# A written order for VectorE and ScalarE in the expert part, and earlier tiles for the first block's second half

## The chip, the core and the metric

The kernel runs on one core of a Trainium2 chip. The metric is the device time of one execution in microseconds (us). The kernel uses all five engines of the core: TensorE (PE; its weight loads are listed as PEld), VectorE (DVE), ScalarE (ACT), GpSimd (POOL) and SyncE (SP), which issues nearly all DMAs here. Each engine works through its own queue of instructions, and semaphores order the engines among each other.

## What is computed

Causal attention over 4 batches, 8 heads, 576 tokens and a head width of 64, mixed with a recalled memory by a gate per head; the result, seen as 2304 tokens of width 512, goes through one gated feed-forward layer of width 1536 ("the expert part"):

```python
def _moe_ref(x, w_gate, w_val, w_out):
    g = x @ w_gate
    silu = g * (1.0 / (1.0 + np.exp(-g)))
    val = x @ w_val
    return (silu * val @ w_out).astype(np.float32)
```

The weights come as 64-bit words that the kernel turns into two 32-bit parts (a high and a low one), and the products are made of three matmuls each: high times high, high times low, low times high.

## The kernel before

**Attention.** A loop over 16 pairs of heads runs the steps named in `STEPS`. Its tiles lie in the pool `sb`, which closes when the loop is over. Each pair's result is stored to two arrays in DRAM, `xdh` and `xdl` (line 640); the last pair's second half is the last store. Beside the attention, `moe1` (lines 220 to 254) does the feed-forward part of four of the twelve weight slices (f = 0 to 3) for the first 1536 tokens. Its tiles are in the pool `mo`, the staging tiles of its weights in the pool `stg`.

**Expert part (from line 693).** Three blocks of 768 tokens, in the order 1536, 0, 768. Each block is two halves of 384 tokens. A unit is one weight slice f on one block. The first block has twelve units: eight plain ones for f = 0 to 3 and 8 to 11 (`eight`, 48 products and 18 sums of 3 products each into the output banks) and four by a seven-product scheme for f = 4 to 7 (`seven`, 42 products and 18). The two other blocks have eight units of `seven` each. So there are 28 units.

- `eight` makes four runs of 12 matmuls: half 0 gate, half 0 value, half 1 gate, half 1 value. Each run fills one of two ring banks in PSUM (tiles `g` and `m`). After a gate run ACT applies Silu (line 923), after a value run DVE multiplies (line 925), ACT rounds to the high part (line 885) and DVE makes the low part (line 114). In the first unit the runs are cut by the pairs of heads, in the order (0, 1), (2), (3), so that they can begin while the last pair is not stored.
- `direct` (line 799) loads the first unit's tokens: `p1` and `p2` are half 0 (tiles `xbh`, `xbl`), `p7` and `p4` are half 1 (tiles in the pool `mb`, which opens on line 781, after `sb` and `mo` are closed).
- `weights2` (line 708) turns a weight slice in three thirds. A third is: a load of 512 KB into one of two tiles `wrawb`, an ACT Prelu (line 714), three DVE operations (lines 715, 721, 722), and where the two parts are wanted at once an ACT copy (line 730) and a DVE subtraction. There are 24 thirds; the units 0 to 7 start three each.
- `operands` (line 744) makes the seven weight combinations of the next unit; `fetch` and `sums` (lines 789, 804) load the next block's tokens and add them; `spread` (line 815) splits the sums into high and low parts.

**What sets the order.** Tile, the planner, orders the instructions of each engine by their priority among those that are ready in its own estimate. The matmuls of the expert part are chained in program order (`inline`). The work of DVE and ACT is not: the conversion, the fetches and the operands have a priority that is later by `LATE` = 60 places, so they are put between the others where the planner sees room. Once planned, each engine runs its queue in that order.

Of the kernel before, what the change touches and what calls it, by code (L numbers as in the profile page):

```python
# [22 lines left out]
NF = DFF // 128  # L23
# [22 lines left out]
TURNS = (4, 5, 8, 9, 10, 11, 6, 7)  # L46
LATE = 60
# [16 lines left out]
def attention_moe(ctx: ExitStack, tc: tile.TileContext, qt, kt_, v, m, beta, wg, wv, wo, out):  # L64
# [135 lines left out]
    def up(ps, f, gv, xh, xl):  # L200
        hi, lo = wsplit[f]
        n = 0
        for kk in range(NPAIR):
            o = gv * 512 + (kk + 2 * gv) % 4 * 128
# [50 lines left out]

    xb = [xbp.tile([128, NPAIR, N2], F32R, name=f"xb{part}") for part in "hl"]
    mo = tc.tile_pool(name="mo", bufs=1, side="right", reuse_waits="tile")
    mo_pool = mo.__enter__()
    stg = tc.tile_pool(name="stg", bufs=1, side="right", reuse_waits="tile")
    stg_pool = stg.__enter__()  # L260
# [4 lines left out]
    with tc.tile_pool(name="sb", bufs=1, reuse_waits="tile") as sb:  # L265
# [385 lines left out]
        def fill(n, k):  # L651
            nonlocal done
            if k == 0:
                for f in WSTEP.get(n, ()):
                    for _ in weights(f, w1, stg_pool, "a", NRAW, 1, loads.get(AFTER[f])):
# [12 lines left out]
        for n in range(NP + 1):  # L668
# [20 lines left out]
        stg.__exit__(None, None, None)  # L689
# [4 lines left out]
    NU = 2 * N2  # L694
    with tc.tile_pool(name="w2", bufs=1, reuse_waits="tile") as w2, \
         tc.tile_pool(name="stg2", bufs=1, reuse_waits="tile") as stg2:
        later = list(range(FC1, NF))
        keep = {}
        for f in later:
            if f < NF - FC1:  # L700
                keep[f] = (
                    w2.tile([128, 1024], F32, name=f"wr{f}"), w2.tile([128, 512], F32R, name=f"woh{f}"),
                    w2.tile([128, 512], F32R, name=f"wol{f}"),
                )
# [3 lines left out]
        def weights2(f):  # L708
            for j, src in enumerate((wg, wv, wo)):
                raw = rot(stg2, "wrawb", [128, 512, 2], I32, 2)  # L710
                SP.dma_start(raw.rearrange("p a b -> p (a b)"), src[f].bitcast(I32))
                top, low = raw[:, :, 1], raw[:, :, 0]
                e = rot(stg2, "web", [128, 512], F32, 2)
                ACT.activation(e, top.bitcast(F32), AF.Prelu, scale=2.0**-111, alpha=2.0**32)  # L714
                DVE.tensor_scalar(e, e, W_TOP * 2.0**-111, -W_TOP * 2.0**-79, op0=ALU.min, op1=ALU.max)  # L715
                c = slice(j * 512, j * 512 + 512)
                if f in keep and j < 2:
                    a = keep[f][0][:, c].bitcast(I32)
                else:
                    a = rot(stg2, "wab", [128, 512], I32, 1)  # L720
                DVE.tensor_scalar(a, e.bitcast(I32), 3, None, op0=ALU.logical_shift_left)
                DVE.scalar_tensor_tensor(
                    out=a, in0=low, scalar=29, in1=a, op0=ALU.logical_shift_right, op1=ALU.bitwise_or
                )
                if f not in keep:
                    oh, ol = (x[:, c] for x in wsplit[f])
                elif j == 2:
                    oh, ol = keep[f][1:]
                if f not in keep or j == 2:
                    ACT.copy(oh, a.bitcast(F32))  # L730
                    split_lo(ol, a.bitcast(F32), oh)
                yield

        def more():
            for f in TURNS:
                yield from weights2(f)

        wgen = more()

        def convert(n):  # L740
            for _ in range(n):
                next(wgen, None)

        def operands(f):

            t = rot(stg2, "tt", [128, 1024], F32, 1)
            if f not in keep:
                bh, bl = wsplit[f]
                w = rot(stg2, "rb", [128, 1024], F32, 1)
                for c in (slice(0, 512), slice(512, 1024)):  # L750
                    DVE.tensor_tensor(w[:, c], bh[:, c].bitcast(F32), bl[:, c].bitcast(F32), op=ALU.add)
            else:
# [3 lines left out]
                for c in (slice(0, 512), slice(512, 768)):  # L756
                    ACT.copy(bh[:, c], w[:, c])
                    DVE.tensor_tensor(bl[:, c], w[:, c], bh[:, c].bitcast(F32), op=ALU.subtract)
            b11, b21, b22, b12 = (w[:, i * 256 : i * 256 + 256] for i in range(4))
            t2, t3, t1, t4 = (t[:, i * 256 : i * 256 + 256] for i in range(4))  # L760
            DVE.tensor_tensor(t1, b12, b11, op=ALU.subtract)
            DVE.tensor_tensor(t2, b22, t1, op=ALU.subtract)
            DVE.tensor_tensor(t3, b22, b12, op=ALU.subtract)
            th = rot(stg2, "th", [128, 1024], F32R, 2)
            tl = rot(stg2, "tl", [128, 1024], F32R, 2)
            for i in range(2):
                c = slice(i * 512, i * 512 + 512)
                if i:
                    DVE.tensor_tensor(t4, b21, t2, op=ALU.subtract)
                ACT.copy(th[:, c], t[:, c])  # L770
                DVE.tensor_tensor(tl[:, c], t[:, c], th[:, c].bitcast(F32), op=ALU.subtract)  # L771
            at = lambda h, l, i: (h[:, i * 256 : i * 256 + 256], l[:, i * 256 : i * 256 + 256])
            return dict(
                p1=at(bh, bl, 0), p2=at(bh, bl, 1), p3=at(bh, bl, 2),
                p6=at(th, tl, 0), p7=at(th, tl, 1), p5=at(th, tl, 2), p4=at(th, tl, 3),
            )

        mo.__exit__(None, None, None)
# [3 lines left out]
        xs = {p: [mbp.tile([128, 2, N2], F32R, name=f"x{p}{part}") for part in "hl"] for p in ("p6", "p7", "p5", "p4", "p3")}  # L782
# [6 lines left out]
        def fetch(t0):  # L789

            got = rot(mbp, "xr", [128, 4, 2, N2], F32, 1)
            for n, (i, j) in enumerate(((1, 0), (1, 1), (0, 0), (0, 1))):
                tmp = rot(mbp, "xt", [128, 2, N2], F32, 1)
                SP.dma_start(got[:, n], block(xdh, t0, i, j))
                SP.dma_start(tmp, block(xdl, t0, i, j))
                DVE.tensor_tensor(got[:, n], got[:, n], tmp, op=ALU.add)
            return [got[:, n] for n in range(4)]

# [5 lines left out]
        def sums(got):  # L804

            a21, a22, a11, a12 = got
            s1 = rot(mbp, "xt", [128, 2, N2], F32, 1)
            s = rot(mbp, "xm", [128, 2, N2], F32, 1)
            DVE.tensor_tensor(s1, a21, a22, op=ALU.add)
            DVE.tensor_tensor(s, s1, a11, op=ALU.subtract)  # L810
            DVE.tensor_tensor(a12, a12, s, op=ALU.subtract)
            DVE.tensor_tensor(a11, a11, a21, op=ALU.subtract)
            return dict(p6=s, p7=a11, p5=s1, p3=a12)

        def spread(mix, p):
            h, l = xs[p]
            for k in range(2):
                ACT.copy(h[:, k], mix[p][:, k])
                DVE.tensor_tensor(l[:, k], mix[p][:, k], h[:, k].bitcast(F32), op=ALU.subtract)

        def tokens(t0, mix):
            direct(t0, "p1", 0, 0)
            direct(t0, "p2", 0, 1)
            for p in ("p6", "p7", "p5"):
                spread(mix, p)
            direct(t0, "p4", 1, 1)
            spread(mix, "p3")
# [5 lines left out]
        chain = [None]  # L833

        def inline(mm):

            if chain[0] is not None:
                follow(mm, chain[0], "products and sums take turns")
            chain[0] = mm

        def product(ps, w, x, start):
            (wh, wl), (xh, xl) = w, x
            n = 0
            for kk in range(2):
                c = slice(kk * 128, kk * 128 + 128)
                for wt, xx in ((wh, xh), (wh, xl), (wl, xh)):
                    inline(PE.matmul(  # L847
                        ps[:, 0:N2], wt[:, c], xx[:, kk, :], start=(start and n == 0), stop=(n == 5), skip_group_check=not start,
                    ))
# [11 lines left out]
        def lower(unit, u, j):  # L861
# [5 lines left out]
            for n, (a, b) in enumerate(((uh, oh), (uh, ol), (ul, oh))):  # L867
                inline(PE.matmul(po[j], a[:, c], b, start=(f == fs[0] and n == 0), stop=(f == fs[-1] and n == 2)))  # L868
            if f == fs[-1]:
                pt = sinks.pop(j)  # L870
                if t0 >= NT1:
                    ACT.mul(pt, po[j], W_ONE)
                else:
                    DVE.scalar_tensor_tensor(out=pt, in0=po[j], scalar=W_ONE, in1=pt, op0=ALU.mult, op1=ALU.add)
# [5 lines left out]
        hold = lambda name, k=2: rot(mbp, name, [128, N2], F32, k)  # L880

        def halves(i, g):
            uh = rot(mbp, f"uh{i}", [128, N2], F32R, 2)
            ul = rot(mbp, f"ul{i}", [128, N2], F32R, 2)
            ACT.copy(uh, g)
            split_lo(ul, g, uh)
            return uh, ul
# [5 lines left out]
        def eight(f, down, begin, back):  # L893
# [163 lines left out]
```

## Time and profile before

| | us |
|---|---|
| three runs | 725.33, 725.62, 728.88 |
| median | 725.62 |
| the profiled execution | 723.74 |
| its span, first to last instruction | 721.9 |
| expert part: first product to the end | 367.8 to 721.9 |
| busy in the span: PE, DVE, ACT | 671.8, 532.0, 405.4 |

The page gives busy time by engine, slices of the span, the chain of work that ended last, and the costliest groups. A busy PE is not PE at its peak, since the ends of matmuls are modelled; the distance from one start to the next is the better measure. Times below are in us from the span's start.

### The profile page before, as it was taken

To read this page: it belongs to the slowest core of one execution; us is meant where nothing else is said; L and a number is where in the kernel's file an instruction comes from. 1 tells how busy PE (TensorE), PEld (TensorE's weight loads), DVE (VectorE), ACT (ScalarE), POOL (GpSimd) and SP (SyncE) were. 2 spreads that over 40 slices of the span, in tenths; PEclk is the share of its full clock that TensorE was granted. 3 is DMA by queue.
4 is the path that set the end of the run, shared out by engine and by line. 5 is a ranking of instruction groups with operands and counts; after the bars stand their busy time and mean duration, and the time that the engine had idled before them with its cause. 6 is when DMAs were issued, how large, how long until landed. Compare 5 with 4: busy or idle time off the path is not lost.

```text
span 721.9 us, 11594 instructions
## 1 busy us (share of the span) xinstructions
PE 671.8 (93%) x4052; PEld 596.4 (83%) x4052; DVE 532.0 (74%) x1302; ACT 405.4 (56%) x889; POOL 193.4 (27%) x252
## 2 busy tenths in 40 slices
PE   4699879999899998999969999999998999999997
PEld 3577768987788886888858999989988999989996
DVE  8999756777786797776625997887787756876544
ACT  5777556677666786666625444445663444544431
POOL 5988764516563456523200000000000000000000
PEclk9899999999899999999988999999999999999999
DMA  9545552123440422312148564440372001610002
GB/s 256 176 148 181 181 188 72 32 88 113 134 160 20 119 90 77 122 55 85 45 145 284 182 195 148 167 139 17 114 245 80 1 1 46 205 56 1 1 1 88
DMA packets 49883, 80.47 MB, mean 111 GB/s; under 512 B 12576, under 2 KB 30496, under 8 KB 49824
## 3 DMA queue, kind: packets, MB, share of 16 engines
q1 hardware_dynamic: 49680, 79.43, 34.6%
q8 instruction: 32, 0.52, 0.3%
q10 hardware_dynamic: 144, 0.29, 0.1%
q14 instruction: 27, 0.22, 0.1%
HBM read 62.40 MB, written 17.30 MB: 110 GB/s over the span
## 4 chain that ended last, share of the span: by engine, by line
PE 53%; DVE 20%; DMA 12%; ACT 5%; issue 5%; POOL 3%; SPq 1%; DVEq 0%; ACTq 0%; POOLq 0%
PE g L847 9%; PE m L847 9%; PE tr L868 5%; PE g L207 4%; PE s L868 4%; PE s L406 3%; PE m L207 3%; PE av L626 3%; PE tr L483 3%; DMA wrawb<-in_wo_dram 2%; DMA xt<-xdl 2%; PE av L868 2%; DMA wrawb<-in_wg_dram 2%; DMA wrawb<-in_wv_dram 2%; PE m L216 1%
## 5 line engine op out<-in xcount | busy, mean ns | idle before, releaser
L420 ACT ACTIVATE pl<-pl,mx 128x384 f32<-128x384 f32 (+1 forms) x64 | 42.6, 667 | 21.5 <-DVE mx L416 21.4
L770 ACT CAST th<-tt 128x512 fp32r<-128x512 f32 x40 | 24.9, 621 | 52.8 <-PE g L847 26.1
L771 DVE TENSOR_TENSOR tl<-tt,th 128x512 fp32r<-128x512 f32 x40 | 27.6, 690 | 32.0 <-ACT th L770 32.0
L459 POOL TENSOR_SCALAR pl<-pl,rs 128x384 f32<-128x384 f32 (+1 forms) x64 | 45.6, 730 | 18.9 <-ACT x L510 12.2
L114 DVE TENSOR_TENSOR g2l<-tr,g2h 128x512 fp32r<-128x512 f32 (+1 forms) x66 | 36.3, 572 | 18.1 <-ACT g2h L465 17.5
L483 PE MATMUL tr<-ident,pl 128*128 128x128 f32 x224 | 38.5, 302 | 6.9 <-POOL pl L459 3.9
L459 POOL TENSOR_SCALAR ps<-ps,rs 128x128 f32<-128x128 f32 (+1 forms) x64 | 28.2, 459 | 58.7 <-DVE rs L456 37.6
L406 PE MATMUL s<-kh,qh 64*128 64x128 f32 (+3 forms) x112 | 26.0, 440 | 17.5 <-DVE mx L416 10.6
L714 ACT ACTIVATE web<-wrawb 128x512 f32<-128x512 f32 x24 | 16.1, 671 | 46.2 <-DMA wrawb<-in_wg_dram 17.9
L416 DVE CUSTOM_DVE_ANT_0 pl<-s,maskp 128x384 f32<-128x384 f32 (+1 forms) x56 | 33.0, 618 | 9.6 <-PE s L406 9.5
L483 PEld LDWEIGHTS tr<-ident,pl 128*128 128x128 f32 x224 | 27.7, 153 | 12.9 <-POOL pl L459 7.7
L465 ACT CAST g2h<-tr 128x512 fp32r<-128x512 f32 (+1 forms) x66 | 30.8, 492 | 7.6 <-PE tr L483 7.2
L420 ACT ACTIVATE ps<-ps,mx 128x128 f32<-128x128 f32 (+1 forms) x64 | 28.8, 452 | 9.9 <-DVE mx L416 9.8
L406 PEld LDWEIGHTS s<-kh,qh 64*128 64x128 f32 x112 | 11.7, 195 | 26.4 <-DVE mx L416 12.3
L510 ACT COPY x<-av 64x256 f32<-64x256 f32 (+1 forms) x44 | 17.3, 393 | 25.4 <-PE av L626 15.8
L626 PE MATMUL av<-g2h,vs 128*128 128x320 f32 (+2 forms) x110 | 30.9, 296 | 0.3 <-ACT g2h L465 0.2
L626 PE MATMUL av<-g2l,vs 128*128 128x320 f32 (+2 forms) x110 | 30.1, 305 | 0.1
L511 DVE TENSOR_TENSOR x<-av,x 64x256 f32<-64x256 f32 (+1 forms) x44 | 19.9, 453 | 12.7 <-ACT x L510 12.1
L378 PE MATMUL tr<-mm,ph 128*128 128x130 f32 x160 | 24.9, 292 | 0.1
L715 DVE TENSOR_SCALAR web<-web 128x512 f32<-128x512 f32 x24 | 10.2, 424 | 20.0 <-ACT web L714 20.0
L114 POOL TENSOR_TENSOR ql<-qr,qh 128x640 fp32r<-128x640 f32 x15 | 24.8, 1654 | 0.1
L612 PE MATMUL av<-g,vz 128*128 128x320 f32 (+2 forms) x100 | 23.0, 380 | 0.6 <-ACT g L330 0.6
(419 smaller groups left out, 2533.5 us busy)
## 6 DMA issues: line engine op xcount, KB each, us to landing
qr<-in_qt_dram SPq DMA_DIRECT2D x16, 384.0 KB, 4.1
xr<-xdh SPq DMA_DIRECT2D x12, 384.0 KB, 3.5
xt<-xdl SPq DMA_DIRECT2D x12, 384.0 KB, 3.9
kr<-in_kt_dram SPq DMA_DIRECT2D x15, 288.0 KB, 3.5
xdh<-xh SPq DMA_DIRECT2D x15, 288.0 KB, 2.6
xdl<-xl SPq DMA_DIRECT2D x15, 288.0 KB, 2.7
wrawb<-in_wg_dram SPq DMA_DIRECT2D x8, 512.0 KB, 3.3
wrawb<-in_wv_dram SPq DMA_DIRECT2D x8, 512.0 KB, 3.7
```

The lines of the kernel that those rows point to most:

```text
L114: return eng.tensor_tensor(dst, src, hi.bitcast(F32), op=ALU.subtract)
L207: PE.matmul(ps, wt[:, c], xx[:, kk, :], start=(n == 0), stop=(n == 11))
L406: mm = PE.matmul(ps[h][:, 0:w], q[rows, t * 128 : t * 128 + 128], k[rows, 0:w], start=(i == 0), stop=(i == 2))
L416: read[id(ps[h])] = DVE.tensor_tensor_reduce(out=p[:, 0:w], in0=ps[h][:, 0:w], in1=maskp[:, 512 - w : 512], op0=ALU.add, op1=ALU.min, scal ...
L420: ACT.activation(p[:, 0:w], p[:, 0:w], AF.Exp, bias=mx[:, c + h : c + h + 1], scale=-1.0, accum_out=self.sm[:, c + h : c + h + 1],)
L459: POOL.tensor_scalar(p, p, rs[:, i : i + 1], 1.0, op0=ALU.mult, op1=ALU.mult)
L465: ACT.copy(view(g[0]), src)
L483: PE.transpose(tr[:, c * 128 : c * 128 + 128], p[:, (k0 + c) * 128 : (k0 + c) * 128 + 128], ident)
L626: PE.matmul(av[:, o:320], self.vs[:, h, kk, :], keys, start=(kk == 0 and g is self.g2[0]), stop=(kk == 4 and g is self.g2[1]),)
L771: DVE.tensor_tensor(tl[:, c], t[:, c], th[:, c].bitcast(F32), op=ALU.subtract)
L847: inline(PE.matmul(ps[:, 0:N2], wt[:, c], xx[:, kk, :], start=(start and n == 0), stop=(n == 5), skip_group_check=not start,))
L868: inline(PE.matmul(po[j], a[:, c], b, start=(f == fs[0] and n == 0), stop=(f == fs[-1] and n == 2)))
```

## The change

- **One order for three engines.** `queued` wraps PE, ACT and DVE: in the expert part each instruction of an engine is chained behind the one before it in the program. `later_by(LATE)` goes. The program now writes down where each piece of work stands: `plan` holds, for each run of `eight` and each step of `seven`, the pieces of conversion, operands, sums and splits that follow it.
- **Thirds.** A third now first makes the low part of the third before, then its DVE operations, then the ACT copy, then the Prelu of the next third, and starts the load of the third after that. The first unit has three thirds, the units 1 to 5 four each, the sixth the last one. In the first unit they stand between the cut runs, ahead of the first Silu. `TURNS`, the order of the slices, changes with it.
- **Tiles.** The weights' staging moves from `stg` to the pool `plain`; when `plain` closes, in the sixth turn of the attention loop, a pool `early` opens with the tiles of `p7` and `p4`. `mo` stays open, and some of its tiles are used again for weights and outputs; so `w2` gets smaller.
- **Smaller things.** Two of the four differences in `operands` become one operation (the gate's rows are permuted in place of the value's); the low parts are made one step later (`halves`); the next block's loads are started from one written place (`sums`), behind the last DVE instruction written before them.

```diff
-TURNS = (4, 5, 8, 9, 10, 11, 6, 7)
-LATE = 60
+TURNS = (4, 5, 8, 6, 9, 10, 11, 7)
...
             if n == len(PLAIN):
                 plain.__exit__(None, None, None)
+                room(ctx.enter_context(tc.tile_pool(name="early", bufs=1, side="right", reuse_waits="tile")), "p7", "p4")
...
+    def queued(eng):
+        class Queued:
+            def __getattr__(self, name):
+                def call(*args, **kw):
+                    ins = getattr(eng, name)(*args, **kw)
+                    if eng in last:
+                        follow(ins, last[eng], "this engine's work is in program order")
+                    last[eng] = ins
+                    return ins
+                return call
+        return Queued()
+    pe, act, dve = queued(PE), queued(ACT), queued(DVE)
...
+        def raw_load(n):
+            if n < len(thirds):
+                f, j = thirds[n]
+                raws[n] = rot(stg2, "wrawb", [128, 512, 2], I32, 2)
+                SP.dma_start(raws[n].rearrange("p a b -> p (a b)"), (wg, wv, wo)[j][f].bitcast(I32))
+        def raw_top(n):
+            if n < len(thirds):
+                tops[n] = rot(stg2, "web", [128, 512], F32, 2)
+                act.activation(tops[n], raws[n][:, :, 1].bitcast(F32), AF.Prelu, scale=2.0**-111, alpha=2.0**32)
...
+        def third(n):
+            while low_parts:
+                a, oh, ol = low_parts.pop()
+                dve.tensor_tensor(ol, a, oh.bitcast(F32), op=ALU.subtract)
...
+            dve.tensor_scalar(e, e, W_TOP * 2.0**-111, -W_TOP * 2.0**-79, op0=ALU.min, op1=ALU.max)
...
+            dve.tensor_scalar(a, e.bitcast(I32), 3, None, op0=ALU.logical_shift_left)
+            dve.scalar_tensor_tensor(
+                out=a, in0=low, scalar=29, in1=a, op0=ALU.logical_shift_right, op1=ALU.bitwise_or
+            )
+            if f not in keep or j == 2:
...
+                act.copy(oh, a.bitcast(F32))
+                low_parts.append((a.bitcast(F32), oh, ol))
+            raw_top(n + 1)
+            raw_load(n + 2)
...
             if begin:
                 for ks in ((0, 1), (2,)):
-                    for i, gv in todo:
+                    for n, (i, gv) in enumerate(todo):
                         run(i, gv, ks)
-            for i, gv in todo:
+                        if n == 3 or ks[0] == 0 and n == 1:
+                            for work in plan.pop(0):
+                                work()
+                plan += [[], [], []]
+            for n, (i, gv) in enumerate(todo):
                 ps = run(i, gv, (3,) if begin else range(NPAIR))
+                halves()
                 if gv == 0:
                     g = hold(("zg", "zh")[i])
-                    ACT.activation(g, ps, AF.Silu, scale=W_ONE)
+                    act.activation(g, ps, AF.Silu, scale=W_ONE)
...
+        raw_load(0)
+        raw_load(1)
+        raw_top(0)
...
+            plan = [[] for _ in range(4 if n < nw else 7)]
+            if n < nw:
+                for k in range(4 if n else 3):
+                    plan[k].append(lambda i=max(0, 4 * n - 1) + k: third(i))
...
+            if n == nw - 2:
+                begin, work, mix = sums(first)
+                begin()
+                for k in range(4):
+                    plan[k] += work[2 * k : 2 * k + 2]
```

## Rows read from the trace of the kernel before

**Rows 1.** The page: busy time, share of the span and instructions by engine.

```profile
PE 671.8 (93%) x4052; PEld 596.4 (83%) x4052; DVE 532.0 (74%) x1302; ACT 405.4 (56%) x889; POOL 193.4 (27%) x252
```

**Rows 2.** Busy time by stretch: length, PE, PEld, DVE, ACT, POOL; clock, DMA share, GB/s.

```profile
371.40:377.10 5.70, 0.01 (x1) 0.01 (x1) 1.47 (x3) 0.87 (x2) 0.00 (x0) 0.78 0.42 136
377.10:384.80 7.70, 6.79 (x19) 5.84 (x20) 0.00 (x0) 0.42 (x1) 0.00 (x0) 0.50 0.97 312
388.40:721.90 333.50, 324.42 (x1680) 297.67 (x1680) 244.24 (x476) 153.55 (x303) 0.00 (x0) 1.00 0.30 97
```

**Rows 3.** PE's waits from 365 on: total us, times, longest.

```profile
PE s L910 <- DMA xp7h<-xdh: 6.6, 2, 5.7
PE g L847 <- DVE zv L946: 1.8, 1, 1.8
PE m L847 <- DVE zg L952: 1.3, 1, 1.3
PE av L868 <- DVE ul L114: 1.2, 1, 1.2
```

**Rows 4.** SP's queue in order of time: start, duration, line, what is loaded or stored.

```profile
332.64 0.32 SPq L640 DMA_DIRECT2D xdl<-xl  x1
...
334.27 0.32 SPq L802 DMA_DIRECT2D xbh<-xdh  x1
...
364.35 0.32 SPq L640 DMA_DIRECT2D xdh<-xh  x1
...
366.10 0.32 SPq L802 DMA_DIRECT2D xbh<-xdh  x1
...
373.38 0.32 SPq L640 DMA_DIRECT2D xdh<-xh  x1
373.91 0.32 SPq L640 DMA_DIRECT2D xdl<-xl  x1
374.32 0.40 SPq L802 DMA_DIRECT2D xp7h<-xdh  x1
...
377.17 0.43 SPq L802 DMA_DIRECT2D xp4h<-xdh  x1
377.64 0.43 SPq L802 DMA_DIRECT2D xp4l<-xdl  x1
378.17 0.38 SPq L711 DMA_DIRECT2D wrawb<-in_wg_dram  x1
```

**Rows 5.** ACT in order of time, up to the first Silu of the expert part.

```profile
384.38 0.67 ACT L714 ACTIVATE web<-wrawb 128x512 f32<-128x512 f32 x1 [11.02 <-DMA wrawb<-in_wg_dram]
385.72 0.68 ACT L714 ACTIVATE web<-wrawb 128x512 f32<-128x512 f32 x1 [0.68 <-DMA wrawb<-in_wv_dram]
386.56 1.28 ACT L923 ACT_TABLE_LOAD   x1
387.85 0.49 ACT L923 ACTIVATE zg<-m 128x384 f32<-128x384 f32 x1
```

**Rows 6.** PE in order of time: neighbours at full clock, 384 and 512 columns.

```profile
385.10 0.34 PE L910 MATMUL s<-xp4h,wl 128*128 128x384 f32 x1
385.27 0.34 PE L910 MATMUL s<-xp4h,wh 128*128 128x384 f32 x1
...
392.89 0.40 PE L868 MATMUL tr<-wl,uh 128*128 128x512 f32 x1
393.12 0.40 PE L868 MATMUL tr<-wh,ul 128*128 128x512 f32 x1
```

**Rows 7.** Groups of DVE and ACT by shape from 366 on: busy us, mean ns.

```profile
L715 DVE TENSOR_SCALAR web<-web 128x512 f32<-128x512 f32 x24 | 10.2, 424 | 20.0 <-ACT web L714 20.0
L722 DVE SCALAR_TENSOR_TENSOR wab<-wrawb,wab 128x512 int32<-128x512 int32 x16 | 11.0, 688 | 0.3
L114 DVE TENSOR_TENSOR ul<-zg,uh 128x384 fp32r<-128x384 f32 x28 | 15.5, 554 | 0.3
L796 DVE TENSOR_TENSOR xr<-xr,xt 128x768 f32<-128x768 f32 x12 | 11.5, 955 | 5.6 <-DMA xt<-xdl 5.0 <-DMA xr<-xdh 0.6
L730 ACT CAST woh<-wab 128x512 fp32r<-128x512 f32 x4 | 2.5, 621 | 2.0 <-DVE wab L722 1.9
```

**Rows 8.** The raw weights' tiles: their loads from issue to landing.

```profile
DMA to landing us min/median/max: 3.1/3.3/7.0
```

More of the change, by code (lines that the diff above doesn't have):

```diff
@@ L705, in attention_moe @@
             else:
                 wsplit[f] = wsplit[f - (NF - FC1)]
[L708 to L742, printed above, removed]
+        thirds = [(f, j) for f in TURNS for j in range(3)]
+        raws, tops = {}, {}
+        def raw_load(n):
[3 more added lines that the diff above has]
+                SP.dma_start(raws[n].rearrange("p a b -> p (a b)"), (wg, wv, wo)[j][f].bitcast(I32))
@@ L744, in operands @@
+        ready = {}
+        slots["th"], slots["tl"] = ([0, [free(f"bx{part}", 0)]] for part in "hl")
         def operands(f):
             t = rot(stg2, "tt", [128, 1024], F32, 1)
[L747 to L752, printed above, removed]
+            th = rot(stg2, "th", [128, 1024], F32R, 2)
+            tl = rot(stg2, "tl", [128, 1024], F32R, 2)
+            raw = f in keep
+            if raw:
@@ L763, in operands @@
[L763 to L772, printed above, removed]
@@ L815, in spread, with sums, load, add @@
-        def spread(mix, p):
-            h, l = xs[p]
[L817 to L827, printed above, removed]
+        def sums(t0):
+            got = rot(mbp, "xr", [128, 4, 2, N2], F32, 1)
+            at = ((1, 0), (1, 1), (0, 0), (0, 1))
+            a21, a22, a11, a12 = (got[:, n] for n in range(4))
+            s1, s = (rot(mbp, name, [128, 2, N2], F32, 1) for name in ("xt", "xm"))
+            tmp = (s, s1)
+            mix = dict(p6=s, p7=a11, p5=s1, p3=a12)
+            def load(n):
+                for dst, src in ((got[:, n], xdh), (tmp[n % 2], xdl)):
+                    ld = SP.dma_start(dst, block(src, t0, *at[n]))
+                    follow(ld, last[DVE], "the loads that come before go first", mybir.DependencyClass.Sync)
+            def add(n):
+                dve.tensor_tensor(got[:, n], got[:, n], tmp[n % 2], op=ALU.add)
+                if n + 2 < 4:
+                    load(n + 2)
+            tt = lambda out, a, b, op: (lambda: dve.tensor_tensor(out, a, b, op=op))
+            work = [lambda n=n: add(n) for n in range(4)] + [
+                tt(s1, a21, a22, ALU.add), tt(s, s1, a11, ALU.subtract), tt(a12, a12, s, ALU.subtract),
+                tt(a11, a11, a21, ALU.subtract),
+            ]
+            return lambda: (load(0), load(1)), work, mix
@@ L928, in eight, with seven, step, rest @@
+                if n:
                     for _ in range(2):
[L929 to L933 removed]
+                        if down:
+                            down.pop(0)()
+            return u
+        def seven(w, down, plan):
+            def step(n, p, start, before=None):
                 ps = bank()
                 product(ps, w[p], xs[p], start)
[L936 removed]
+                return ps[:, 0:N2]
+            def rest(n):
+                for work in plan[n]:
+                    work()
+                if n and down:
@@ L948, in seven @@
-            ACT.activation(g2, g2, AF.Silu, scale=W_ONE)
-            val = step("p3", False)
-            u = []
-            for i, (g, v) in enumerate(((g1, val), (g2, v2))):
-                DVE.scalar_tensor_tensor(out=g, in0=v, scalar=W_ONE, in1=g, op0=ALU.mult, op1=ALU.mult)
-                u.append(halves(i, g))
+            u = [None, None]
+            act.copy(p1, step(0, "p1", True))
+            halves()
+            rest(0)
+            dve.tensor_tensor(g1, step(1, "p2", True), p1, op=ALU.add)
@@ L962, in attention_moe @@
             direct(first, "p4", 1, 1, (k,))
-        ready = {}
-        last = None
+        raw_load(0)
+        raw_load(1)
+        raw_top(0)
+        before = None
+        spreads = lambda mix, *what: [
+            (high if kind == "h" else low)(mix, p, k) for kind, p in what for k in range(2)
+        ]
+        arrive = []
         for n, unit in enumerate(units):
```

249 lines of the change are left out of this document (144 added, 105 removed).

## Prediction

> **What bounds the kernel now.** I read the page's busy times first: PE is busy for 93% of the span, DVE for 74%, ACT for 56% [rows 1]. So PE is the bound, and only time in which PE stands or runs slowly can be won; the number of matmuls does not change. Then I looked at what PE waited for from the end of the attention on. The list falls into two parts [rows 3]. One wait is for the loads of p7, 6.6 us, at the seam between attention and experts. All others follow the first unit: 1.8, 1.3 and 1.2, with three smaller ones 5.7 in all. A record's modelled end lies 0.17 us beyond the next start [rows 6], so each of those six stalls cost about 0.17 more: 6.7 us, an estimate. Busy time by stretch confirms it: from 388.4 to the end PE is busy for 324.4 of 333.5 us [rows 2], with the end of the program in the rest. The seam is dearer than its wait: PE stands from 371.4 to 377.1, and then the granted clock is 0.50 (1.2 GHz) until 384.8, where it is otherwise 1.00 (2.4 GHz) [rows 2]. Unit 1 begins only at 388.4, when the first Silu has freed its bank: a Silu that comes after two Prelus and a table load of 1.28 us [rows 5].
>
> So the most that the change can win is some 9 us at the seam and 6.7 behind it.
>
> **Part 1, the early tiles.** p7 holds pairs 12 and 13. Their last store was issued at 332.6, the same pairs' p1 was loaded at 334.3, yet p7 was issued at 374.3, right behind the attention's last stores [rows 4], and PE waited for it. Nothing it reads was late. What p7 has in common with the raw weights, which come behind it at 378.2, is a pool that opens after `sb` closes: the planner queues such loads behind the last users of `sb`. A pool that opens in mid attention takes p7 and half of p4 out of there; they can be issued with p1. The last pair's part of p4 still needs the last store. From such a store to the load that needs it took 1.75 us (364.35 to 366.10) [rows 4], so it is issued at 373.38 + 1.8 = 375.2, before 377.2, and lands some 2.5 us later at 377.7 to 378.2.
>
> PE's own path then: at 371.4 twelve of the 48 matmuls of unit 0 are done as today; 30 more need no late data, 30 x 0.172 = 5.2 us [rows 6], to 376.6; the last six follow their load, to about 379.2. Taken alone this would start unit 1 at 379.2 in place of 388.4, 9.2 us earlier.
>
> **Part 2, the written order at the seam.** Unit 1 needs the bank of run 0, so it needs the first Silu. In the new program order ACT has ahead of that Silu: Prelu 0, 1 and 2, the copy of third 2, and Prelu 3. These hang on loads, and `stg2` still opens after `sb` closes. By the same row pattern the raw loads stand behind the last stores and behind the rest of p4: issue at about 376.2 and 376.6, two p4 loads earlier in the burst. At 3.3 us to land [rows 8] the first is there at L = 379.4. From there: Prelu 0, 0.67 [rows 5]; third 0 on DVE, 0.42 + 0.42 + 0.69 = 1.53 and 0.1 between queues [rows 7]: L + 2.3. Only now can load 2 reuse the tile: landing at L + 5.65. Prelu 2, third 2, copy (0.67 + 1.6 + 0.65): L + 8.6. Prelu 3 (0.67), table load (1.28), Silu (0.49) [rows 5]: L + 11.05. That is 390.5, against 388.4: **2.1 us later**, though PE is ready at 379.2. It begins at 389 if the raw loads are queued ahead of p4, and at 392 if PE's filling work delays the last head, so 0.5 to 4; I add 0.5 for the second and take 2.6.
>
> PE would stand for 11 us, longer than the 5.7 after which the clock was at half for 7.7 us [rows 2]. In the old seam most of that slow stretch lay before the Silu and cost little; now it falls on unit 1, where PE is the bound. Four to 7.7 us at half speed cost 2.0 to 3.8; I take **2.7**. The seam is then 5.3 us worse.
>
> Here a rule speaks against the change as well: the Trainium skill ("PSUM — Partial Sum Buffer", section "Engine vs sequencer instructions") says that ScalarE and VectorE queues are strict FIFO. By that rule the Silu cannot pass a Prelu that waits for its load. The trace of before agrees as far as it goes: ACT stands 11.02 us before a Prelu [rows 5], and nothing passes it.
>
> **Part 3, the units behind.** A unit of `eight` takes 48 x 0.172 + 18 x 0.233 = 12.45 us of PE [rows 6]. Units 1 to 5 now have four thirds. A third with both parts costs DVE 1.53 + 0.69, and each run has one more 0.55: 2.8 x 4 = 11.1 us [rows 7], which fits. Load to load, two thirds take 3.3 + 0.67 + 1.6 = 5.6 us against 6.2 of PE. That fits too, but narrowly. I take no cost; a bank may be late by 4.9 us (a run and the sums on both sides of it) before PE notices.
>
> At units 6 and 7 the first token sums stand in DVE's queue, and their loads begin only behind unit 5's last DVE instruction, some 1.2 us before run 0 of unit 6 ends. Two sums of 0.95 [rows 7] wait for 1.5 MB, then the next two for loads that can start only afterwards; the multiplication that frees PE's bank is behind them. At the 312 GB/s of the seam's burst [rows 2] run 3 of unit 6 is late by 0.3 and run 1 of unit 7 by 2.0; at 260, by 1.3 and 2.9. I take **3.0** (2.3 to 4.2). The sum would be smaller by a page's figure: the Trainium skill ("DMA: Bandwidth & Descriptors", "Specifications") gives about 358 GB/s of HBM per core, with which the two would come to about 1.5; the burst's row decides.
>
> In `seven` a step takes 1.7 us, a bank may be late by 2.4, and the written pieces depend on steps before. Operands cost DVE 4.0 to 4.3 us a unit, the unit's own work 3.9, of 11.4: no stall in an ordinary unit. The stalls of 1.8, 1.3 and 1.2 lay where sums and evacuations met at the ends of blocks [rows 3]; the written order spreads the sums over three units. In the first unit of the third block DVE has about 14.5 us of work in 11.4, so I leave **1.0** (0 to 3). The fused difference saves 0.15 us of DVE a unit, beside PE: nothing.
>
> **The sum.** Seam +2.6 + 2.7; stalls behind it -6.7, own stalls +3.0 + 1.0: **+2.6 us**, 726.3 against the profiled execution's 723.74. That execution lies 1.9 under the median of the runs (725.62), so the same step on the median is 728.2; I say 727. Bounds of the terms: +0.5 + 2.0 + 2.3 - 6.7 = -2 and +4 + 3.8 + 4.2 + 3 - 6.7 = +8, so 722 to 733.
>
> **Rivals.**
> 1. *The raw loads are early.* If the planner puts loads 0 and 1 into SP's idle time before 373, the thirds run beside the attention's end and the Silu waits for nothing. Then unit 1 begins at 379.2: -9.2 - 2.7 = about -12, 712 to 715. For it: SP is idle for long stretches there, and the loads lose their late priority. Against it: p7 had no late priority either and was not moved [rows 4].
> 2. *The queue bites in every unit (slower).* The 5.6 us for two thirds include no disorder on SP or DMA. Where a load takes 4.4 in place of 3.3 us, two thirds take 6.7 against PE's 6.2, and ACT's Silu stands behind the late Prelu. Over 20 thirds that is 5 us, with the 4.9 of slack once off, and the third block's first unit 2 us more: +6 to +12, 731 to 737. It decides from a landing of about 3.9 us; the range of rows 8 goes to 7.0.
> 3. *The early tiles bring nothing by themselves*, though they are loaded early: that is contained in the forecast, since the Silu decides.
>
> **Chances.** Forecast 0.70, rival 1 0.17, rival 2 0.13. Within the forecast's 722 to 733 I put 0.04 under -0.5%, 0.47 within and 0.19 above; 0.5% (3.6 us) is about what a measurement of this kernel can tell from no change. So faster 0.21, same 0.47, slower 0.32. To leave out no more than 0.2, the range goes from 714, inside rival 1, to 735.
>
> **What would show it.** Right: in the new trace p7 is issued before 340, wrawb only after 373.9; ACT shows four Prelus and a table load ahead of the first Silu, which ends near 390; PE stands some 11 us up to unit 1 and runs at 0.50 afterwards; around unit 7 PE waits for a DVE multiplication behind the token sums; the waits at the ends of blocks are gone. Wrong: wrawb issued before 370, or the first Silu before 380 (rival 1); PE waits in each of units 1 to 5 (rival 2).

## The result, and the profile after

The changed kernel takes 732.25 us (median of 6 runs, 730.71 to 732.90) against 725.58 of the kernel before, run beside it (6 runs). The ratio is 1.0078, 95% interval 1.0055 to 1.0101: **slower by 0.8%**. The profiled execution took 732.83 us with a span of 731.0, that is 9.1 more than the span before. (Executions of one program differ by some us, and so does their mean granted clock: 29 later runs of the kernel before gave 720.8 to 728.8 us at mean clocks of 0.965 to 0.983, and one run of e4_sums_earlier, 840.5 us at 0.744, is in no median below. So places inside a trace are compared from the attention's last store on, or from the last store of pair 13 where the attention's end may have moved, and whole kernels by medians.)

First the page's busy line. PE's work is what it was in [rows 1]; its share of the longer span fell from 93% to 92%.

```profile
PE 673.5 (92%) x4052; PEld 599.6 (82%) x4052; DVE 535.3 (73%) x1282; ACT 405.4 (55%) x889; POOL 192.3 (26%) x252
```

What PE waited for from 365 on (total us, times, longest), to be held against [rows 3]. L703 is the helper through which all work of PE, ACT and DVE in the expert part now goes, so the tiles tell what is meant.

```profile
PE m L703 <- ACT zg L703: 13.0, 1, 13.0
PE s L703 <- DMA xp4h<-xdh: 3.2, 1, 3.2
PE g L703 <- DVE zh L703: 2.2, 1, 2.2
PE m L703 <- DVE zg L703: 2.1, 1, 2.1
PE g L703 <- DVE zg L703: 1.2, 1, 1.2
PE av L703 <- DVE ul L703: 0.6, 1, 0.6
```

The wait for p7, 6.6 us before, is gone. In its place PE waits 3.2 us for the rest of p4 and then 13.0 us for the first Silu, which frees the bank of unit 1's first run. The other four are the stalls behind the seam, the stretch between attention and experts; they are looked at below.

SP's queue in order of time (start, duration, what), beside [rows 4]:

```profile
333.65 0.32 SPq L642 DMA_DIRECT2D xdl<-xl  x1
...
335.29 0.32 SPq L831 DMA_DIRECT2D xbh<-xdh  x1
335.65 0.45 SPq L831 DMA_DIRECT2D xp7h<-xdh  x1
...
377.11 0.32 SPq L642 DMA_DIRECT2D xdl<-xl  x1
378.38 0.32 SPq L831 DMA_DIRECT2D xp4h<-xdh  x1
...
379.28 0.42 SPq L740 DMA_DIRECT2D wrawb<-in_wg_dram  x1
...
387.15 0.33 SPq L740 DMA_DIRECT2D wrawb<-in_wo_dram  x1
```

p7 is now loaded beside p1, at 335.65 in place of 374.3. The raw weights still come behind the last stores, and those are 3.2 us later than before.

ACT up to the first Silu of the expert part, beside [rows 5] (in brackets: idle time before, and what ended it):

```profile
384.77 0.66 ACT L703 ACTIVATE web<-wrawb 128x512 f32<-128x512 f32 x1 [8.21 <-DMA wrawb<-in_wg_dram]
385.94 0.67 ACT L703 ACTIVATE web<-wrawb 128x512 f32<-128x512 f32 x1 [0.51 <-DMA wrawb<-in_wv_dram]
390.48 0.66 ACT L703 ACTIVATE web<-wrawb 128x512 f32<-128x512 f32 x1 [3.86 <-DMA wrawb<-in_wo_dram]
392.82 0.62 ACT L703 CAST woh<-wab 128x512 fp32r<-128x512 f32 x1 [1.68 <-DVE wab L703]
393.34 0.65 ACT L703 ACTIVATE web<-wrawb 128x512 f32<-128x512 f32 x1
394.02 1.28 ACT L703 ACT_TABLE_LOAD   x1
395.31 0.49 ACT L703 ACTIVATE zg<-m 128x384 f32<-128x384 f32 x1
```

Four Prelus (the ACT step of a third), a copy and the table load stand ahead of the Silu, and ACT waits 8.2 us ahead of the first and 3.9 us ahead of the third of them for loads. The Silu's own bank had been full since about 377.

Busy time by stretch (PE, PEld, DVE, ACT, POOL, then clock, DMA share, GB/s), beside [rows 2]:

```profile
382.40:395.80 13.40, 0.49 (x2) 0.00 (x0) 4.55 (x9) 4.94 (x7) 0.00 (x0) 0.50 0.49 166
395.80:399.00 3.20, 3.15 (x10) 3.15 (x11) 2.01 (x4) 1.41 (x4) 0.00 (x0) 0.50 0.00 0
395.80:731.00 335.20, 324.64 (x1680) 300.10 (x1680) 246.53 (x451) 151.68 (x301) 0.00 (x0) 0.99 0.29 96
```

**Where the 9.1 us came from.** Unit 1 begins at 395.8 in place of 388.4: 7.4. From there to the end it takes 335.2 in place of 333.5: 1.7, of which the half clock at the start is 1.4 (10 matmuls in 3.15 us that take 1.7 at full clock). So the stalls behind the seam cost about as much as the old ones, where the forecast had them 2.7 cheaper. Of the 7.4, 1.0 stands already in the last store of pair 13 (333.65 against 332.64), which the change does not move; the seam itself is 6.4 us longer.

### The profile page after: what moved, and what is told of

Read it like the earlier page. It is cut to its first block, busy times and chain, and to the rows that moved or that the text cites. A ratio compares the mean times of both kernels' runs of the same rounds, so it can differ in the third digit from the quotient of the medians.

```text
span 731.0 us, 11570 instructions
## 1 busy us (share of the span) xinstructions
PE 673.5 (92%) x4052; PEld 599.6 (82%) x4052; DVE 535.3 (73%) x1282; ACT 405.4 (55%) x889; POOL 192.3 (26%) x252
## 4 chain that ended last, share of the span: by engine, by line
PE 65%; DVE 14%; DMA 8%; ACT 5%; issue 4%; POOL 3%; SPq 0%; DVEq 0%; ACTq 0%; POOLq 0%
PE g L703 13%; PE m L703 13%; PE tr L703 7%; PE s L703 5%; PE g L206 4%; PE s L408 3%; PE m L206 3%; PE tr L485 3%; PE av L628 3%; PE av L703 2%; DMA xt<-xdl 1%; PE m L215 1%; DVE ph L372 1%; PE m L216 1%; PE m L217 1%
## 5 line engine op out<-in xcount | busy, mean ns | idle before, releaser
L113 DVE TENSOR_TENSOR g2l<-tr,g2h 128x512 fp32r<-128x512 f32 (+1 forms) x66 | 36.4, 572 | 18.7 <-ACT g2h L467 18.2
L485 PE MATMUL tr<-ident,pl 128*128 128x128 f32 x224 | 40.0, 310 | 6.8 <-POOL pl L461 4.5
L418 DVE CUSTOM_DVE_ANT_0 pl<-s,maskp 128x384 f32<-128x384 f32 (+1 forms) x56 | 33.0, 618 | 10.9 <-PE s L408 10.8
L703 ACT ACTIVATE zh<-zh 128x384 f32<-128x384 f32 x20 | 10.5, 526 | 34.2 <-DVE zh L703 34.2
L703 PE MATMUL m<-xbh,wh 128*128 128x384 f32 x48 | 17.0, 354 | 13.0 <-ACT zg L703 13.0
L703 ACT CAST uh<-zh 128x384 fp32r<-128x384 f32 x28 | 14.4, 514 | 25.4 <-DVE zh L703 25.2
L703 ACT ACTIVATE web<-wrawb 128x512 f32<-128x512 f32 x24 | 16.0, 665 | 20.3 <-DMA wrawb<-in_wg_dram 8.5
```

The source lines that it names most:

```text
L113: return eng.tensor_tensor(dst, src, hi.bitcast(F32), op=ALU.subtract)
L418: read[id(ps[h])] = DVE.tensor_tensor_reduce(out=p[:, 0:w], in0=ps[h][:, 0:w], in1=maskp[:, 512 - w : 512], op0=ALU.add, op1=ALU.min, scal ...
L485: PE.transpose(tr[:, c * 128 : c * 128 + 128], p[:, (k0 + c) * 128 : (k0 + c) * 128 + 128], ident)
L703: ins = getattr(eng, name)(*args, **kw)
```

## The experiments

One table holds the places that the readings below compare. "To unit 1" is the time from the last store's issue to unit 1's first product, and "from pair 13" the time to it from the last store of pair 13; "unit 1 on" is from that product to the end of the span. All but the medians are read from one profiled execution of each kernel. The kernel before, run again beside the experiments, kept its median (725.58, 725.77, 725.51).

| kernel | last store | first Prelu | first Silu ends | to unit 1 | from pair 13 | unit 1 on | median us (runs) |
|---|---|---|---|---|---|---|---|
| before | 373.91 | 384.38 | 388.34 | 14.5 | 55.75 | 333.5 | 725.58 (6) |
| changed | 377.11 | 384.77 | 395.80 | 18.7 | 62.20 | 335.2 | 732.25 (6) |
| e1_silu_first | 375.01 | 383.15 | 376.26 | 5.3 | 48.75 | 337.9 | 722.67 (10) |
| e2_order_alone | 372.67 | 384.27 | 395.15 | 22.5 | 63.73 | 337.0 | 734.64 (4) |
| e3_silu_first_no_early | 374.66 | 391.69 | 388.98 | 15.2 | 56.38 | 337.0 | 733.27 (4) |
| e4_sums_earlier | 375.74 | 383.42 | 394.32 | 18.6 | 62.06 | 334.5 | 729.94 (11) |
| e5_hold_back | 374.00 | 381.41 | 392.33 | 18.4 | 59.65 | 336.6 | 731.08 (6) |
| e6_raw_early | 374.52 | 116.51 | 391.12 | 16.7 |  | 335.3 | 727.90 (10) |
| e8_raw_first | 375.20 | 379.57 | 390.47 | 15.3 | 58.78 | 338.3 | 728.89 (10) |
| e7_all_three | 371.85 | 379.26 | 374.59 | 5.3 | 46.53 | 330.6 | 710.69 (6) |

(In e6_raw_early the attention itself runs otherwise, with the last store of pair 13 at 340.45; so that place is empty.)

### The thirds out of the first unit

```diff
-                        if n == 3 or ks[0] == 0 and n == 1:
-                            for work in plan.pop(0):
-                                work()
-                plan += [[], [], []]
...
-        raw_top(0)
         before = None
...
-            if n < nw:
-                for k in range(4 if n else 3):
-                    plan[k].append(lambda i=max(0, 4 * n - 1) + k: third(i))
+            if n == 0:
+                plan[3].append(lambda: raw_top(0))
+            if 0 < n < 6:
+                for k in range(4):
+                    plan[k].append(lambda i=4 * n - 4 + k: third(i))
+            if n == 6:
+                plan[0].append(lambda: third(20))
+                plan[1].append(lambda: third(99))
+            if n in (8, 9, 10):
+                plan[3].append(lambda i=n + 13: third(i))
+            if n == 11:
+                plan[3].append(lambda: third(99))
```

(`third(99)` makes only the low part that is still due.)

> The changed kernel with one thing undone: unit 0 has no thirds, and Prelu 0 stands behind unit 0's work. Units 1 to 5 do the thirds 0 to 19, unit 6 the third 20, and the last three (f = 7, not needed before unit 11) stand one each in units 8 to 10. Theory A (the loss is the first Silu, queued on ACT behind Preludes whose loads are late): PE begins unit 1 some 1.5 us after the last p4 load lands at 381.3, so at 382.5 to 383.5 in place of 395.8, without a half-clock stretch behind it; the time falls by 13 + 1.5 to about 717 to 719. Theory B (the loss is the written order in the units themselves, with the seam only uncovering it): the thirds now start without a lead, PE waits for them in units 1 to 5, and the time stays at 724 to 730. Theory C (the loss is the last head, put behind products of p7): seam as in A only if the Silu is the last thing that PE waits for; otherwise 729 to 732.

ACT of this kernel:

```profile
374.48 1.28 ACT L703 ACT_TABLE_LOAD   x1
375.77 0.49 ACT L703 ACTIVATE zg<-m 128x384 f32<-128x384 f32 x1
...
383.15 0.67 ACT L703 ACTIVATE web<-wrawb 128x512 f32<-128x512 f32 x1 [1.47 <-DMA wrawb<-in_wg_dram]
384.13 0.49 ACT L703 ACTIVATE zg<-m 128x384 f32<-128x384 f32 x1 [0.32 <-PE m L703]
```

The Silu runs before the first raw weight has landed, and unit 1 begins 5.3 us after the last store, right behind unit 0's last product. That is 13.4 us less than in the changed kernel, with the loads just as late: the seam's loss is the Silu's place in ACT's queue. Theory B falls for units 1 to 5: PE waits in none of them. The median is 722.67, ratio to before 0.9958 (0.9935 to 0.9981), a gain of 9.6 where 13 to 15 were expected. One missing part is the half clock, which was expected to go: it still falls on unit 1, for 10 matmuls (about 1.5 us). The other is in unit 6:

```profile
PE g L703 <- DVE zg L703: 4.0, 1, 4.0
```

```profile
453.60:457.60 4.00, 0.07 (x1) 0.00 (x0) 2.37 (x4) 0.00 (x0) 0.00 (x0) 0.76 0.65 225
457.60:461.60 4.00, 3.92 (x12) 3.93 (x13) 1.58 (x3) 0.90 (x2) 0.00 (x0) 0.50 0.88 307
```

The same wait was 1.2 in the changed kernel. Here the sums' loads are issued between the last two raw loads and take 7.6 us for the first pair, where they took 4.5 in the changed kernel; and after standing 4.4 us PE runs at the half clock once more.

### Early tiles and written order apart

One edit takes the early tiles away: from the changed kernel it makes e2_order_alone, from e1_silu_first it makes e3_silu_first_no_early.

```diff
-                room(ctx.enter_context(tc.tile_pool(name="early", bufs=1, side="right", reuse_waits="tile")), "p7", "p4")
...
-        room(mbp, "p6", "p5", "p3")
+        room(mbp, "p6", "p7", "p5", "p4", "p3")
```

> The changed kernel without the early pool: p7 and p4 lie in the pool that opens after the attention, as in the kernel before. The written order stays. Theory A (the Silu chain decides, the early tiles bring nothing by themselves): PE waits for p7 as before, some 6 us, but the first Silu still ends near 396, since the raw loads are issued behind the same last stores (2.2 us earlier, as no products of p7 stand ahead of the last head) and behind four loads more; 730 to 733, the same as the changed kernel. Theory B (the early tiles save their 6 to 9 us in any case): 738 to 741. Theory C (the last head's delay is the loss): 2.2 less than the changed kernel, 729.5 to 730.5, and the Silu ends near 393.5.

> e1_silu_first without the early pool. Theory A: with the Silu free, the products of unit 0 decide; p7 is loaded after the last stores, PE stands for it some 6 us and runs at the half clock as in the kernel before, and unit 1 starts at 387 to 389; 722 to 724, 4 to 7 us more than e1_silu_first. So the early tiles would be worth 4 to 7 us here, and nothing in e2_order_alone. Theory B (the early tiles bring nothing in any order): the same time as e1_silu_first within 1.5 us. Theory C (the tiles' worth is the same with and without the thirds ahead of the Silu): the difference to e1_silu_first equals that of e2_order_alone to the changed kernel.

What PE waited for in e2_order_alone:

```profile
PE m L702 <- ACT zg L702: 7.9, 1, 7.9
PE s L702 <- DMA xp7h<-xdh: 7.0, 2, 6.8
```

The order alone is 9 us slower than before (ratio 1.0136, 1.0100 to 1.0172). The Silu ends at 395.2, near the 396 of theory A, but the time lies 1.6 above A's range and below B's 738. Adding the early tiles to it wins 2.4 (734.64 to 732.25). Adding them where the Silu is free wins 10.6 by the medians (733.27 to 722.67) and 8.7 between the profiled runs. So the tiles' worth depends on what is late next, and theory C of e3_silu_first_no_early is out. It is not zero under the late Silu either: without p7 and half of p4 in the burst, the raw loads are issued 2.2 us after the last store and not 5.5.

From the last store to unit 1 the tiles save 9.9 us where the Silu is free. From pair 13 they save 7.6, since they also put the last store itself 2.2 later, as the next experiment shows.

The time of e3_silu_first_no_early missed its expectation by 10, which the trace explains in part only. The seam is as expected (15.2), and the stretch behind costs 337.0, with a stall in unit 6 and the half clock after it, as in e1_silu_first. But the profiled run, 728.63, is the fastest of the four; the others took 731.4 to 735.7 at mean clocks of 0.969 and 0.960 against its 0.978, and no trace shows where.

### The last head

```diff
+                if self.n == NP - 1:
+                    tail.append(end)
...
+                        if ks[0] == 0 and n == 2:
+                            last[PE] = tail[0], last[PE]
                         run(i, gv, ks)
```

(`end` is the attention's last product; the chain takes both entries of such a pair as forerunners.)

> The changed kernel, with the first product of p7 chained behind the last product of the attention; nothing else differs. Theory A: the last head's products start 2.2 us earlier (13 matmuls of 0.172 fewer ahead of them), the last stores are issued 2.2 earlier, and with them the rest of p4, the raw loads, Prelu 0 and the first Silu; 729.5 to 730.5. Theory B (the last head is not what the raw loads wait for): the Silu stays at 395.8 and the time at 732.

PE's queue in the changed kernel at the last head:

```profile
370.89 0.34 PE L703 MATMUL s<-xp7h,wh 128*128 128x384 f32 x1
...
372.97 0.34 PE L703 MATMUL m<-xbh,wh 128*128 128x384 f32 x1
373.15 0.32 PE L628 MATMUL av<-g2h,vs 128*128 128x320 f32 x1
```

From 370.89 to 373.15 twelve products of p7 and one of p2 stand ahead of the last head's first: 2.26 us. With the edit the last store comes 41.3 us after pair 13's last store, as it did before, in place of 43.5. That much of theory A holds, and unit 1 begins 2.5 us sooner from pair 13. The median fell by 1.2 only, to above A's range, and the times alone do not show a gain: the ratio to before is 1.0081 (1.0053 to 1.0110), against the changed kernel's 1.0078. In this profile the half clock lasts longer (14 matmuls) and comes again after the stall in unit 7 (10), 2.1 us more in all.

### The raw loads

The early pool given to the raw and Prelu tiles in place of p7 and p4:

```diff
+                early = ctx.enter_context(tc.tile_pool(name="early", bufs=1, side="right", reuse_waits="tile"))
+                slots["wrawb"] = [0, [early.tile([128, 512, 2], I32, name=f"wrawb{i}") for i in range(2)]]
+                slots["web"] = [0, [early.tile([128, 512], F32, name=f"web{i}") for i in range(2)]]
```

> The early pool holds the two raw tiles and the two Prelu tiles in place of p7 and p4, which go into the late pool; all else as in the changed kernel, so it stands beside e2_order_alone (734.64), which has neither early. Theory A (a load is late because its tile's pool opens after the attention's pool is closed): the first two raw loads are issued in mid attention, before 350, Prelu 0 and 1 no longer wait, and what is left ahead of the Silu is load 2 (behind p4's loads, landing near 384 to 385), Prelu 2, third 2, copy, Prelu 3, table load: the Silu ends at 389 to 391 in place of 395.2, and the time is 728.5 to 731. Theory B (raw loads are late by their place in the program, not by their pool): they are still issued behind 373, the Silu stays near 395, 734 to 735.

```profile
101.23 0.42 SPq L742 DMA_DIRECT2D wrawb<-in_wg_dram  x1
```

With the tiles in a pool that opens in mid attention the same two loads, at the same place of the program, are issued from 101 on in place of 379: lateness comes from the pool. The Silu's chain then waits for load 2 alone and ends at 391.1, as expected; the time is 727.9, 6.7 below e2_order_alone and 0.6 below the expected range.

Raw loads 0 and 1 ahead of p4's last two on SP's queue:

```diff
-                SP.dma_start(raws[n].rearrange("p a b -> p (a b)"), (wg, wv, wo)[j][f].bitcast(I32))
+                last["raw"] = SP.dma_start(raws[n].rearrange("p a b -> p (a b)"), (wg, wv, wo)[j][f].bitcast(I32))
...
-        for k in range(2):
-            direct(first, "p2", 0, 1, (k,))
-            direct(first, "p4", 1, 1, (k,))
+        direct(first, "p2", 0, 1, (0,))
+        direct(first, "p4", 1, 1, (0,))
+        direct(first, "p2", 0, 1, (1,))
         raw_load(0)
         raw_load(1)
+        p4_rest = [
+            SP.dma_start(dst[:, 1].bitcast(F32), block(src, first, 1, 1)[:, 1])
+            for dst, src in zip(xs["p4"], (xdh, xdl))
+        ]
+        for ld in p4_rest:
+            follow(ld, last["raw"], "the raw weights go first")
```

> The changed kernel with the first two raw loads ahead of the last two loads of p4 on SP's queue. Theory A (the raw loads took 5.4 and 6.1 us because they share the burst with p4's two loads): the first lands some 2 us sooner after the last stores, so do Prelu 0 and the Silu; p4 lands later, but still well before the Silu; 730 to 730.5. Theory B (they are slow by themselves, two loads at once): the same time as the changed kernel within 1 us, as only 1.0 us of issue is won: 731 to 732.

```profile
375.20 0.32 SPq L642 DMA_DIRECT2D xdl<-xl  x1
375.61 0.40 SPq L740 DMA_DIRECT2D wrawb<-in_wg_dram  x1
...
376.56 0.42 SPq L1021 DMA_DIRECT2D xp4h<-xdh  x1
```

```profile
379.57 0.66 ACT L703 ACTIVATE web<-wrawb 128x512 f32<-128x512 f32 x1 [4.92 <-DMA wrawb<-in_wg_dram]
...
389.98 0.49 ACT L703 ACTIVATE zg<-m 128x384 f32<-128x384 f32 x1
```

From its issue to Prelu 0 the first load now takes 4.0 us, in the changed kernel 5.5. The Silu ends 15.3 us after the last store in place of 18.7, though p4 lands later. That is theory A, with 3.4 us won at the seam where 2 were expected, as the load is also issued 1.8 us nearer to the store. The median, 728.89, is as much lower; but the profiled run took 730.61, as unit 1 on costs 3.1 more there, with the half clock for 15 matmuls in unit 1 and 8 in unit 7.

### The token sums

```diff
+            if n == nw - 3:
+                begin, due, mix = sums(first)
+                plan[2].append(begin)
             if n == nw - 2:
-                begin, work, mix = sums(first)
-                begin()
-                for k in range(4):
-                    plan[k] += work[2 * k : 2 * k + 2]
+                plan[0] += due[0:2]
+                plan[2] += due[2:4]
+                plan[3] += due[4:8]
```

> The changed kernel with the first block's token sums started earlier: their first loads are issued behind unit 5's third run (before: at unit 6's start), the first two sums stand in unit 6's first run, the next two in its third, the four differences in its fourth. Theory A (the two stalls at units 6 and 7, 1.43 and 2.40 us beyond a normal step, come from DVE standing before these loads): both go, 3.8 us, so 728 to 729 against the changed kernel's 732.25. Theory B (the loads only move their wait: they delay the last raw loads, or the second pair of sums still waits): a wait of 1 to 3 us stays in units 5 to 7, 730 to 732. Theory C (the loss there is DVE's amount of work, not its waiting): the stalls stay, 732.

DVE of the changed kernel, and then of this one:

```profile
468.92 0.96 DVE L703 TENSOR_TENSOR xr<-xr,xt 128x768 f32<-128x768 f32 x1 [2.49 <-DMA xt<-xdl]
469.80 0.55 DVE L703 SCALAR_TENSOR_TENSOR zg<-g,zg 128x384 f32<-128x384 f32 x1
...
474.64 0.96 DVE L703 TENSOR_TENSOR xr<-xr,xt 128x768 f32<-128x768 f32 x1 [2.69 <-DMA xt<-xdl]
```

```profile
466.48 0.96 DVE L703 TENSOR_TENSOR xr<-xr,xt 128x768 f32<-128x768 f32 x1 [1.05 <-DMA xt<-xdl]
467.36 0.55 DVE L703 SCALAR_TENSOR_TENSOR zg<-g,zg 128x384 f32<-128x384 f32 x1
...
473.84 0.96 DVE L703 TENSOR_TENSOR xr<-xr,xt 128x768 f32<-128x768 f32 x1 [1.99 <-DMA xt<-xdl]
```

The first stall is gone, of the second 1.2 of 2.4 us stay, since the second pair's loads can start only when the first pair is added. So the waiting is the cause and theory C is out; 2.6 of the 3.8 us go. It is the trace that shows this. The median is 729.94, 2.3 lower and in theory B's range, but the ratio to before, 1.0060 (1.0033 to 1.0087), overlaps the changed kernel's, and in this profile the half clock lasts 16 matmuls in unit 1 and comes again in the third block.

### All three together

The thirds out of unit 0, the last head ahead of p7, the sums earlier; no other edit.

> e1_silu_first, e4_sums_earlier and e5_hold_back together: no thirds in unit 0, the sums started earlier, the last head ahead of p7's products. If the three terms add up: from e1_silu_first's 722.67 the last head's 2.2 (PE's wait for the rest of p4, 3.3 us there, shrinks by as much) and the 4.4 of its stall at unit 6 less 0.2; 715.5 to 718.5. If the earlier sums only move their wait (theory B of e4_sums_earlier): 719 to 721. If the seam's gain was partly a lucky draw of the clock: 720 or more.

```profile
PE g L706 <- DVE zh L706: 1.3, 1, 1.3
PE m L706 <- DVE zg L706: 1.3, 1, 1.3
PE s L706 <- DMA xp4h<-xdh: 1.1, 1, 1.1
...
```

```profile
375.60:377.20 1.60, 1.44 (x7) 1.19 (x8) 0.56 (x1) 0.54 (x2) 0.00 (x0) 1.00 0.82 278
377.20:381.00 3.80, 3.80 (x24) 3.80 (x23) 2.10 (x5) 2.23 (x5) 0.00 (x0) 1.00 0.41 153
```

710.69 us, ratio to before **0.981** (0.9775 to 0.9846): faster than both kernels, and 5 to 8 us better than the sum of the terms. PE never stands longer than 1.7 us at the seam or behind it, and the clock stays at 1.00 there. e1_silu_first lost time at the half clock in two places (10 and 14 matmuls), which no term of that sum had counted; they are worth about 3.5 us. The profiles agree: from pair 13 to the end e7_all_three takes 9.5 us less than e1_silu_first, 2.2 up to unit 1 and 7.3 behind it, of which 4.2 were the stall that the sum had counted. The rest of the medians' difference is within what executions differ by.

## Why the prediction was right and where it was wrong

- **Which loads move: right.** p7 came with p1 and the raw weights stayed behind the last stores. That the pool is the reason was argued from rows; e6_raw_early shows it.
- **The chain from the first landing to the Silu: right.** It was worked out as 11.05 us from landing. From Prelude 0's start to the Silu's end the changed kernel took 11.0, and e2_order_alone, e4_sums_earlier, e5_hold_back and e8_raw_first took 10.9 each, with the landing 5 us apart. The Trainium skill's rule ("PSUM — Partial Sum Buffer", "Engine vs sequencer instructions", strict FIFO queues) agrees with the trace: the Silu had its data at 377 and ran at 395.3.
- **The landing itself: mis-sized, by 5.4 us (379.4 against 384.8).** This term was the furthest off and made the forecast too low. Three parts. One us is there already at pair 13's store (333.65 against 332.64); this store lies between 330.7 and 333.7 in the experiments where the attention is the same, so it is no effect of the change. 2.2 us are p7's products ahead of the last head, for which the prediction had 0.5: it counted the 30 products that were free to run, and did not ask where they would stand in PE's queue. 2.2 us are the load: 3.3 to land was the median of all 24 [rows 8], while the first raw load of before, at the very place, was issued at 378.17 [rows 4] and ended ACT's wait at 384.38 [rows 5]. The nearest row said 6.2, and the load took 5.5.
- **The early tiles' 9.2 us: right behind the last store, but they cost 2.2 of it ahead of it.** They were to bring unit 1 to 5.3 us behind the last store; with the Silu free it was 5.3. From pair 13, though, unit 1 begins 7.0 us sooner than before in e1_silu_first, and the whole 9.2 sooner only in e7_all_three, where the last head stands ahead of p7. Under the late Silu the tiles brought 2.4 and not nothing.
- **The half clock: 1.4 in place of 2.7, and under its lower bound of 2.0.** It did fall on unit 1, for 3.1 us. How long it lasts is partly a draw: behind the late Silu it took 10 matmuls here, 11 in e6_raw_early, and 14 to 17 in e2_order_alone, e4_sums_earlier, e5_hold_back and e8_raw_first (an estimate of 2.1 to 2.5 us).
- **Units 1 to 5: right,** no stall; rival 2 did not happen there. The raw loads' longest landing, 6.1 us, was the seam's.
- **Units 6 and 7: 3.8 (1.4 and 2.4) in place of 3.0,** in the places and by the cause named. The first four loads, 1.57 MB, took from 461.0 to 468.9: 199 GB/s. The DMA as a whole moved 237 GB/s in that stretch, as the next pair's first loads had begun; both are less than the 260 to 312 of the estimate. The Trainium skill ("DMA: Bandwidth & Descriptors", "Specifications") gives about 358 GB/s of HBM per core, by which the term would have been about 1.5, an estimate; these loads did not come near it.
- **Blocks' ends: the old stalls went, new ones came at the third block's first unit: 3.0 in place of 1.0.** That is the upper end of the term's bounds. The prediction had DVE's amount of work; the rows show a wait for the partial outputs, with the multiplications that free PE's banks behind it. No run took that wait away, so this cause is read and not tested.

```profile
639.92 0.69 DVE L703 SCALAR_TENSOR_TENSOR o<-tr,o 128x512 f32<-128x512 f32 x1 [1.53 <-DMA o<-part]
640.53 0.55 DVE L703 SCALAR_TENSOR_TENSOR zh<-zv,zh 128x384 f32<-128x384 f32 x1
...
642.73 0.69 DVE L703 SCALAR_TENSOR_TENSOR pt<-tr,pt 128x512 f32<-128x512 f32 x1 [1.19 <-DMA pt<-part]
```

- **The old stalls: 6.7 was 0.6 too much.** The six waits include the 0.4 with which unit 1 begins, at 388.4, and which ends with the Silu: it belongs to the seam. The five behind it cost 6.1.
- **The sum.** Forecast: seam +2.6, clock +2.7, stalls -6.7 + 3.0 + 1.0 = +2.6. Measured: +7.4, +1.4, -6.7 + 3.8 + 3.0 = +8.9 of the profiled 9.1 (with 6.1 for the old stalls, +9.5). The mechanism was the right one; 4.8 of the 6.3 us that were missing are the seam's, and 1.0 of those is the attention's place in this execution. So the time fell inside the range (714 to 735) and 5 us above the forecast, on the slower side and not within 0.5%. That it also lies inside the forecast's own 722 to 733 is partly luck: the seam's term was outside its bounds of 0.5 to 4, and the profiled step of 9.1 is above the upper sum of +8. The median moved by 6.7 only, because the profiled execution of before was 1.8 under its median and this one 0.6 above.

## What to carry to other kernels

When an order is written by hand, look at what each engine's queue holds ahead of the one instruction that frees the bottleneck's next buffer: optional work that hangs on a late load must stand behind it. An early buffer is worth only what the next late thing leaves, so cost it together with that thing, and ask what the work that it sets free will delay. Measure such a gain from a place that the change cannot move. Take a transfer's time from the row at the same place, in the same burst, and not from the median of all.

## What the runs showed of the hardware beyond that

After short stands of PE its granted clock fell to 0.50 (1.2 GHz) in some cases and not in others. (A stand is the time from one product's start to the next one's.) It fell in e1_silu_first after 3.7 us (for 10 matmuls) and after 4.4 us (14), and after the stands of 12.9 to 13.5 us at the seam (10 to 16). After 1.4 and 1.7 us in e7_all_three it stayed at 1.00. In unit 7 it fell after 2.3 us in e5_hold_back (10), 2.1 us in e2_order_alone (11) and 2.9 us in e8_raw_first (8), but not after 2.6 us in the changed kernel and 2.3 us in e6_raw_early. In the third block it fell after 2.2 us in e4_sums_earlier and not after 2.4 us in the changed kernel. At the half clock a matmul of 384 columns takes 0.32 us from start to start in place of 0.17. So a stall of 2 to 4.5 us can cost 1.2 to 2.1 us more, an estimate from these counts, and part of the spread between executions of one program may come from there; the runs do not settle how much.
